# Order edges for the weight decoding of a fused attention and two-layer expert kernel

## The chip, the cores and the metric

The kernel runs on one core of a Trainium2 chip. The metric is the device time of one execution in microseconds. A core has five engines that each work through their own instructions in order: TensorE (PE; its weight loads are shown apart as PEld), VectorE (DVE), ScalarE (ACT), GpSimd (POOL) and SyncE (SP), which issues the DMAs. An engine waits for another through semaphores.

## The reference

Attention over 2 batches, 8 heads, 576 positions and 64 channels, in two parts that are added; a gated layer; a layer of four experts:

```
q_d, k_d, v_d = means of q, k, v over groups of 4 positions
out_up    = repeat(softmax(scale * q_d @ k_d.T) @ v_d, 4)
scores    = where(|i - j| < 4, scale * q @ k.T, -1e9)
x = out_up + softmax(scores) @ v           # 1152 tokens x 512

h = x @ w_in                               # 512 x 2048
x = (h * sigmoid(h)) @ w_out               # 2048 x 512

p = domain_probs / sum(domain_probs)       # 1152 x 4
out = sum over e of p[:, e] * (relu(x @ w1[e]) @ w2[e])    # 512 x 1024, 1024 x 512
```

## The kernel before

**Precision.** Each float32 operand of a large product is kept as two halves, h and l, of TensorE's fast type: h is the rounded value (a copy by ScalarE), l the difference (a subtraction by VectorE or GpSimd). A product is three matmuls, h·h, h·l, l·h (`mm3`).

**Attention** is 16 jobs (2 batches, 2 ranges of 256 and 320 queries, 4 pairs of heads), spread over ticks, three ticks from one job to the next. A job's instructions are: scores L303 and L327 on TensorE; maximum L316, L317, exponent L321, sum L324, downsampled maximum L341 to L343; normalising L348 to L353; transposes L363, L365; values L391, L395; the sum o (L400), and the two halves of x, xh (L407, ScalarE) and xl (L408, VectorE). Four jobs make one chunk of tokens; chunks have 256, 320, 256 and 320 tokens.

**Layer one** has two halves of 1024 hidden channels (`hf`), four chunks each, and in each chunk eight first steps (`g1_step`: 12 matmuls at L468, evacuated by L487 on ScalarE, L488 on VectorE and, one step later, by L493 and L494) and four second steps (`g2_step`: 24 matmuls at L468, evacuated by L520 in the first half, by L523, L525 and a ScalarE copy in the second). The attention of later chunks runs among the steps of earlier ones.

**Weights of layer one** come as eight units (0 to 7) of four pieces. Units 0 and 1 are the first weights of half 0, units 2 and 3 its second weights. A piece is loaded into one of three `stg` buffers and decoded (`split_raw`): two ScalarE steps (L165, L166), two VectorE steps on `dec` (L167, L169; `dec` has two buffers), h by ScalarE (L171), l by GpSimd (L172). When a piece has been taken, the next load is given out. Units 8 and 9, two pieces each, are plain float32, the first half of expert 0's weights: h by L175, l by L176. The text counts units from one where it says "units two to four", which are 1 to 3 in the code; pieces are counted from one, so units 1 to 3 are pieces 5 to 16.

**Layer two** goes through four experts, four chunks and four steps. First products are again L468 (`m1_products`), evacuated by L644; sums `r` (L649), their halves L651 and L652; then seven products at L667 on weights in the form of sums: `ks` (L568) holds sums of the raw weights `kst`, and `split_kk` makes halves of sums and weights (L596, L598).

**What sets the order.** The code is written in program order with a priority for each instruction (`prio`, `at_prio`; ticks and steps are its unit), and a scheduler with a model of the engines' times places instructions on the engines by priority and readiness. A piece is decoded at priority `needed(u, j) - LEAD_SPLIT` and loaded at `needed(u, j) - LEAD_LOAD`; `SPLIT_AT` says at which ticks of the attention the first ten pieces are called. Later pieces are called by `split_ok` after a step, as long as their unit is under `limit`. A manual edge without a semaphore ("NoSync") only says that an instruction stands behind another one.

## Time and profile before

| | |
|---|---|
| Runs | 705.44, 707.71, 708.93 us; median 707.71 |
| Profiled execution | 708.98 us, its span from first to last instruction 707.20 us |
| Granted TensorE clock, mean | 0.984 of full speed |
| PE busy | 668.5 us (95%) |
| PEld busy | 649.8 us (92%) |
| DVE busy | 445.1 us (63%) |
| ACT busy | 332.6 us (47%) |
| POOL busy | 248.9 us (35%) |
| DMA | 48.16 MB |

In the trace the first chunk's steps end near 98.7 us, the third chunk begins near 148, the second half of layer one near 212, layer two near 312, and the last products near 700. A busy time by stretch gives for each engine the busy microseconds and, in brackets, the number of instructions; PEclk is the granted TensorE clock as a share of full speed. In a timeline or a chain the columns are start, length, engine, line, operation, tiles and shapes; neighbouring instructions of one kind are joined (x2), and a bracket says how long the engine had been idle before and which engine, tile and line released it. A mean over a line is over instructions with different neighbours.

### The profile page before, as it was taken

The numbers are of one execution on the slowest core, as the hardware profiler recorded it, in microseconds if no ns is written. First come the engines' busy times: TensorE is split into PE (matmuls) and PEld (weight loads), VectorE is DVE, ScalarE is ACT, GpSimd is POOL, SyncE is SP. The second block draws the span as 40 slices with busy tenths as digits, with TensorE's granted clock in tenths as the row PEclk, the third lists the DMA queues.
The fourth block names the chain that finished last, engine by engine and source line by source line (L and its number), as shares of the span: only waits on it lengthen the run. The fifth ranks groups of instructions, "written<-read, shape, count | busy, mean of one in ns | idle before, by whom it ended". The sixth has DMA issues, their size and how long they took to land.

```text
span 707.2 us, 13791 instructions
## 1 busy us (share of the span) xinstructions
PE 668.5 (95%) x5516; PEld 649.8 (92%) x5516; DVE 445.1 (63%) x882; ACT 332.6 (47%) x753; POOL 248.9 (35%) x346
## 2 busy tenths in 40 slices
PE   5777999999989999998999999999999999999996
PEld 4565899999889999998999999999999999999995
DVE  5988747546864434674555886538866559755444
ACT  4667646457763422543334643335533356433321
POOL 4574442114420000365324482136542244322210
PEclk9978999999999999999999999999999999999999
DMA  9875532005461000032001420003210010000001
GB/s 260 246 220 196 164 94 64 22 12 168 137 201 32 1 1 1 1 123 87 1 1 33 139 69 1 1 1 112 99 31 1 1 53 9 1 32 16 17 31 44
DMA packets 16927, 48.16 MB, mean 68 GB/s; under 512 B 2976, under 2 KB 4256, under 8 KB 16864
## 3 DMA queue, kind: packets, MB, share of 16 engines
q1 hardware_dynamic: 16864, 47.29, 21.4%
q8 instruction: 43, 0.70, 0.4%
q14 instruction: 20, 0.16, 0.1%
HBM read 44.93 MB, written 2.36 MB: 67 GB/s over the span
## 4 chain that ended last, share of the span: by engine, by line
PE 79%; DMA 8%; DVE 6%; ACT 3%; issue 2%; POOL 2%; SPq 0%; DVEq 0%; POOLq 0%; ACTq 0%
PE mm L468 49%; PE p L667 25%; DMA stg<-in_w_dram 5%; DVE dec L169 2%; DMA kst<-in_w2d_dram 2%; DVE dec L167 1%; PE s L303 1%; POOL wbuf L172 1%; DMA vg<-in_va_dram 1%; PE o L395 1%; PE t L363 1%; ACT dec L165 1%; PE o L391 1%; DVE gl L494 1%; ACT stg L166 1%
## 5 line engine op out<-in xcount | busy, mean ns | idle before, releaser
L468 PE MATMUL mm<-xh,wbuf 128*128 128x256 f32 (+2 forms) x1280 | 274.6, 299 | 5.5 <-ACT xh L407 2.8
L468 PEld LDWEIGHTS mm<-xh,wbuf 128*128 128x128 f32 x1280 | 214.2, 192 | 7.2 <-DVE gf L488 3.6
L468 PE MATMUL mm<-xl,wbuf 128*128 128x256 f32 (+2 forms) x640 | 191.0, 299 | 0.0
L649 POOL TENSOR_TENSOR r<-r 128x128 f32<-128x128 f32 x160 | 93.5, 595 | 190.9 <-ACT r L644 150.9
L652 DVE TENSOR_TENSOR h<-r,h 128x384 fp32r<-128x384 f32 (+1 forms) x128 | 89.8, 702 | 72.5 <-ACT h L651 72.2
L468 PEld LDWEIGHTS mm<-xl,wbuf 128*128 128x128 f32 x640 | 122.5, 191 | 0.3
L651 ACT ACTIVATE h<-r 128x384 fp32r<-128x384 f32 (+1 forms) x128 | 73.9, 578 | 87.2 <-POOL r L649 57.2
L468 PE MATMUL mm<-gh,wbuf 128*128 128x256 f32 (+1 forms) x512 | 104.7, 297 | 0.9 <-ACT acc L520 0.9
L667 PE MATMUL p<-wext,h 128*128 128x256 f32 x672 | 96.1, 284 | 2.4 <-ACT h L651 2.4
L667 PEld LDWEIGHTS p<-wext,h 128*128 128x128 f32 x672 | 87.6, 191 | 2.8 <-ACT h L651 2.8
L667 PE MATMUL p<-wbuf,h 128*128 128x256 f32 x672 | 85.4, 280 | 0.0
L468 PEld LDWEIGHTS mm<-gh,wbuf 128*128 128x128 f32 x512 | 82.6, 188 | 1.2 <-ACT acc L520 1.2
L667 PEld LDWEIGHTS p<-wbuf,h 128*128 128x128 f32 x672 | 82.0, 188 | 0.0
L468 PE MATMUL mm<-gl,wbuf 128*128 128x256 f32 (+1 forms) x256 | 74.6, 297 | 0.0
L644 ACT ACTIVATE r<-mm 128x512 f32<-128x512 f32 x48 | 28.6, 597 | 82.4 <-PE mm L468 82.4
L649 DVE TENSOR_TENSOR r<-r 128x128 f32<-128x128 f32 x96 | 33.4, 348 | 40.7 <-ACT r L644 36.3
L494 DVE TENSOR_TENSOR gl<-gf,gh 128x256 fp32r<-128x256 f32 (+1 forms) x64 | 35.9, 562 | 19.6 <-ACT gh L493 19.4
L468 PEld LDWEIGHTS mm<-gl,wbuf 128*128 128x128 f32 x256 | 47.8, 188 | 0.1
L172 POOL TENSOR_TENSOR wbuf<-dec,wbuf 128x512 fp32r<-128x512 f32 x24 | 32.4, 1354 | 33.1 <-ACT wbuf L171 26.0
L598 POOL TENSOR_TENSOR wext<-kst,wext 128x512 fp32r<-128x512 f32 x8 | 10.6, 1325 | 85.0 <-issue 72.9
L695 DVE SCALAR_TENSOR_TENSOR acc<-p,pr,acc 128x256 f32<-128x256 f32 (+1 forms) x63 | 36.3, 604 | 6.5 <-PE p L667 6.5
L493 ACT ACTIVATE gh<-gf 128x256 fp32r<-128x256 f32 (+1 forms) x64 | 28.2, 441 | 19.0 <-DVE gf L488 19.0
(122 smaller groups left out, 989.0 us busy)
## 6 DMA issues: line engine op xcount, KB each, us to landing
stg<-in_w_dram SPq DMA_DIRECT2D x32, 512.0 KB
kst<-in_w2d_dram SPq DMA_DIRECT2D x16, 512.0 KB
kst<-in_w1d_dram SPq DMA_DIRECT2D x12, 512.0 KB
kq<-in_kqa_dram SPq DMA_DIRECT2D x8, 419.0 KB
kq<-in_kqb_dram SPq DMA_DIRECT2D x8, 323.0 KB
vg<-in_va_dram SPq DMA_DIRECT2D x8, 288.0 KB
stg<-in_w1d_dram SPq DMA_DIRECT2D x4, 512.0 KB
vw<-in_vb_dram SPq DMA_DIRECT2D x8, 180.0 KB
```

Of the source, the lines that this page charges most:

```text
L169: DVE.scalar_tensor_tensor(out=ai, in0=v[:, :, 1], scalar=-2 ** 31, in1=ai, op0=ALU.bitwise_and, op1=ALU.bitwise_or)
L172: POOL.tensor_tensor(out=l[:, c], in0=a, in1=h[:, c].bitcast(F32), op=ALU.subtract)
L468: ins = [PE.matmul(out=ps, lhsT=l, rhs=r, start=(first and i == 0), stop=(last and i == n - 1)) for i, (l, r) in enumerate(pairs)]
L493: ACT.activation(out=gh[ft][:, 0:n], in_=gf[:, 0:n], func=ACTF.Copy)
L494: DVE.tensor_tensor(out=gl[ft][:, 0:n], in0=gf[:, 0:n], in1=gh[ft][:, 0:n].bitcast(F32), op=ALU.subtract)
L598: eng.tensor_tensor(out=l[:, r], in0=x, in1=h[:, r].bitcast(F32), op=ALU.subtract)
L644: ACT.activation(out=r[:, 0:4].rearrange("p s t -> p (s t)"), in_=ps[:, 0:512], func=ACTF.Relu)
L649: (DVE if k in FAST_K and o != 7 else POOL).tensor_tensor(out=r[:, o], in0=r[:, a], in1=r[:, b], op=op)
L651: ACT.activation(out=h, in_=r[:, part], func=ACTF.Copy)
L652: DVE.tensor_tensor(out=l, in0=r[:, part], in1=h.bitcast(F32), op=ALU.subtract)
L667: ins = [PE.matmul(out=ps, lhsT=x, rhs=y, start=(opens and k == 0 and i == 0), stop=(k == 3 and i == n - 1), skip_group_check=True) for i, ...
L695: DVE.scalar_tensor_tensor(out=o, in0=ps, scalar=p, in1=o, op0=ALU.mult, op1=ALU.add)
```

## The change

In the first chunk the pieces of units 1 to 3 get other priorities (`needed`), other ticks (`SPLIT_AT`), and an edge: their first VectorE step stands behind the xl subtraction (L408) of an attention job, behind job 2's for unit 1 and behind job 3's for units 2 and 3 (jobs count from 0). In the second half, the pieces of units 8 and 9 are no longer called at the end of the fourth chunk of half 0 but behind odd first steps of the second chunk of half 1, and what counts as background (these pieces, the sums `ks`, the weight halves of expert 0's last two steps) gets an edge behind the running step's last evacuation on its engine (`latest`, `behind`). The sums `ks` are no longer made as soon as a buffer is free in `stage_ahead` but called by name in `sum_ahead`: expert 0's together with the weight halves, a later expert's in the third chunk and behind `split_kk`.

```diff
-SPLIT_AT = (-14, -11, -8, -6, -5, -5, -4, -3, -2, -1)
+SPLIT_AT = (-14, -11, -8, -6, -4, -4, -4, -4, -1, -1)
...
-            return (4, 8, 8, 48, 52, 56, 56)[u - 1]
+            return (-5, -2, 2, 48, 52, 56, 56)[u - 1]
...
+    latest = {}
+    def follow(i, earlier, reason):
+        tc.add_manual_dep(i.ins, earlier.ins.name, mybir.DependencyInfo(mybir.DependencyClass.NoSync, mybir.DependencyReason.DATA),
+                          reason=reason)
+    def behind(eng, i):
+        if eng in latest:
+            follow(i, latest[eng], "background work")
+        return i
...
-            DVE.scalar_tensor_tensor(out=ai, in0=ai, scalar=3, in1=v[:, :, 0],
-                                     op0=ALU.logical_shift_left, op1=ALU.bitwise_or)
+            i = DVE.scalar_tensor_tensor(out=ai, in0=ai, scalar=3, in1=v[:, :, 0],
+                                         op0=ALU.logical_shift_left, op1=ALU.bitwise_or)
+            if u in behind_job:
+                follow(i, behind_job[u], "first weights")
...
-            ACT.activation(out=h[:, c], in_=t, func=ACTF.Copy)
-            DVE.tensor_tensor(out=l[:, c], in0=t, in1=h[:, c].bitcast(F32), op=ALU.subtract)
+            behind(ACT, ACT.activation(out=h[:, c], in_=t, func=ACTF.Copy))
+            behind(DVE, DVE.tensor_tensor(out=l[:, c], in0=t, in1=h[:, c].bitcast(F32), op=ALU.subtract))
...
+        if j.i < 4:
+            behind_job.update({1: i} if j.i < 3 else {2: i, 3: i})
...
-        while sums_todo and sums_todo[0] in staged and ks_p and len(sums) < 2:
+    def sum_ahead(e, k):
+        if (e, k) in ((e, k) for e, x, k in sums_todo):
+            assert sums_todo[0] == (e, "k", k) and len(sums) < 2
...
-                    eng.tensor_tensor(out=o, in0=a, in1=b, op=ALU.subtract)
+                    behind(eng, eng.tensor_tensor(out=o, in0=a, in1=b, op=ALU.subtract))
...
+                if e == 0 and k > 1:
+                    behind(ACT, a)
+                    behind(eng, b)
...
-                split_ok(limit[0])
+                if hf == 1 and ci == 1 and ft % 2:
+                    limit[0] = 10
+                    split_ok(10)
+                elif limit[0] < 10:
+                    split_ok(limit[0])
...
-                for k in range(2):
-                    split_kk(0, k)
+                for k in range(4):
+                    sum_ahead(0, k)
+                    if k < 2:
+                        split_kk(0, k)
...
-                limit[0] = 8 if hf == 0 else 10
+                limit[0] = 8
...
-            if hf == 0 and ci == 3:
-                limit[0] = 10
...
             split_kk(e + 1, k)
+            if k < 2:
+                sum_ahead(e + 1, k + 2)
...
+                if ci == 2 and k % 2 == 0 and e < NE - 1:
+                    sum_ahead(e + 1, k // 2)
```

`latest` is set at L493, L494, L525 and its ScalarE copy, L649 and L652. The order listings below give instructions of one engine in the order in which they stand, with the numbers of the tiles; an instruction's line in after is its line there (L167 and L169 become L180 and L184, L176 becomes L191, L488 and L494 become L504 and L510, L523 and L525 become L539 and L541, L568 becomes L587, L598 becomes L617, L649 becomes L672, L652 becomes L675).

**VectorE, attention of jobs 0 to 2.** `dec` tiles are decoding steps; `o_249` is the sum of job 0, `o_434` of job 2. Before:

```order
L169 SCALAR_TENSOR_TENSOR dec_501<-stg64_403,dec_501 128x512
L167 SCALAR_TENSOR_TENSOR dec_542<-dec_542,stg64_485 128x512
L169 SCALAR_TENSOR_TENSOR dec_542<-stg64_485,dec_542 128x512
L400 TENSOR_TENSOR o_249<-o_249,od_262 128x256
L167 SCALAR_TENSOR_TENSOR dec_590<-dec_590,stg64_499 128x512
L169 SCALAR_TENSOR_TENSOR dec_590<-stg64_499,dec_590 128x512
L341 TENSOR_REDUCE st_280<-s_270 128x1
L408 TENSOR_TENSOR xl_74<-o_249,xh_73 128x256
```

After, on the same engine, from job 0's sum, and from job 2's:

```order
L414 TENSOR_TENSOR o_249<-o_249,od_262 128x256
L422 TENSOR_TENSOR xl_74<-o_249,xh_73 128x256
L355 TENSOR_REDUCE st_280<-s_270 128x1
...
L414 TENSOR_TENSOR o_434<-o_434,od_447 128x256
L355 TENSOR_REDUCE st_467<-s_455 128x1
L330 TENSOR_REDUCE st_593<-s_581 128x5
L356 TENSOR_SCALAR st_467<-st_467 128x1
L422 TENSOR_TENSOR xl_74<-o_434,xh_73 128x256
L180 SCALAR_TENSOR_TENSOR dec_524<-dec_524,stg64_327 128x512
```

The decoding steps that stood around job 0's sum and halves are gone from there; the first of units 1 to 3 (`stg64_327`) now stands behind job 2's xl.

**VectorE, end of half 0's decoding.** `dec_2625` is the last piece of unit 7, `gf_2648` the first evacuation of half 1, the L176 are pieces of units 8 and 9. Before:

```order
L169 SCALAR_TENSOR_TENSOR dec_2625<-stg64_2579,dec_2625 128x512
L176 TENSOR_TENSOR wbuf_76<-stg_2588,wbuf_76 128x1024
L176 TENSOR_TENSOR wbuf_76<-stg_2623,wbuf_76 128x1024
L176 TENSOR_TENSOR wbuf_76<-stg_2632,wbuf_76 128x1024
L488 SCALAR_TENSOR_TENSOR gf_2648<-th_2647,mm_2634 128x256
L176 TENSOR_TENSOR wbuf_76<-stg_2653,wbuf_76 128x1024
L494 TENSOR_TENSOR gl0_85<-gf_2648,gh0_77 128x256
```

After, the same place, and then the first two pieces of units 8 and 9 in the second chunk of half 1:

```order
L184 SCALAR_TENSOR_TENSOR dec_2625<-stg64_2579,dec_2625 128x512
L504 SCALAR_TENSOR_TENSOR gf_2648<-th_2647,mm_2634 128x256
L510 TENSOR_TENSOR gl0_85<-gf_2648,gh0_77 128x256
...
L510 TENSOR_TENSOR gl0_85<-gf_2916,gh0_77 128x320
L191 TENSOR_TENSOR wbuf_76<-stg_2588,wbuf_76 128x1024
L504 SCALAR_TENSOR_TENSOR gf_2933<-th_2932,mm_2919 128x320
L504 SCALAR_TENSOR_TENSOR gf_2956<-th_2955,mm_2942 128x320
L510 TENSOR_TENSOR gl1_86<-gf_2933,gh1_78 128x320
L510 TENSOR_TENSOR gl2_87<-gf_2956,gh2_79 128x320
L191 TENSOR_TENSOR wbuf_76<-stg_2623,wbuf_76 128x1024
```

Four subtractions of 128x1024 have left the place ahead of half 1's first two evacuations and stand one chunk later.

**VectorE and GpSimd, seam of the layers.** L598 are weight halves of expert 0, L523 and L525 the last two evacuations of layer one, L652 the first halves of layer two. VectorE before:

```order
L523 SCALAR_TENSOR_TENSOR gf_3733<-mm_3708,acc_75 128x320
L598 TENSOR_TENSOR wbuf_76<-ks_3630,wbuf_76 128x256
L525 TENSOR_TENSOR xl_74<-gf_3733,xh_73 128x320
L598 TENSOR_TENSOR wbuf_76<-ks_3630,wbuf_76 128x512
L598 TENSOR_TENSOR wbuf_76<-kst_2722,wbuf_76 128x512
L598 TENSOR_TENSOR wbuf_76<-ks_3645,wbuf_76 128x256
L598 TENSOR_TENSOR wbuf_76<-ks_3645,wbuf_76 128x512
L523 SCALAR_TENSOR_TENSOR gf_3762<-mm_3737,acc_75 128x320
L598 TENSOR_TENSOR wbuf_76<-kst_3628,wbuf_76 128x512
L525 TENSOR_TENSOR xl_74<-gf_3762,xh_73 128x320
L652 TENSOR_TENSOR h1_3822<-r_3820,h0_3821 128x384
```

VectorE after:

```order
L539 SCALAR_TENSOR_TENSOR gf_3733<-mm_3708,acc_75 128x320
L541 TENSOR_TENSOR xl_74<-gf_3733,xh_73 128x320
L539 SCALAR_TENSOR_TENSOR gf_3762<-mm_3737,acc_75 128x320
L541 TENSOR_TENSOR xl_74<-gf_3762,xh_73 128x320
L617 TENSOR_TENSOR wbuf_76<-ks_3640,wbuf_76 128x512
L617 TENSOR_TENSOR wbuf_76<-kst_3066,wbuf_76 128x512
L617 TENSOR_TENSOR wbuf_76<-ks_3640,wbuf_76 128x256
L617 TENSOR_TENSOR wbuf_76<-ks_3645,wbuf_76 128x512
L617 TENSOR_TENSOR wbuf_76<-kst_3623,wbuf_76 128x512
L617 TENSOR_TENSOR wbuf_76<-ks_3645,wbuf_76 128x256
L675 TENSOR_TENSOR h1_3812<-r_3810,h0_3811 128x384
```

The six weight halves stood between the evacuations of the last two steps and now stand behind both.

GpSimd before; `ks_3800` and `ks_3815` are sums for expert 1:

```order
L598 TENSOR_TENSOR wbuf_76<-kst_3628,wbuf_76 128x512
L649 TENSOR_TENSOR r_3820<-r_3820 128x128 x4
L649 TENSOR_TENSOR r_3857<-r_3857 128x128 x3
L568 TENSOR_TENSOR ks_3800<-kst_3786 128x256
L568 TENSOR_TENSOR ks_3815<-kst_3798 128x256
L649 TENSOR_TENSOR r_3857<-r_3857 128x128
L568 TENSOR_TENSOR kst_3786<-kst_3786 128x256
```

GpSimd after:

```order
L617 TENSOR_TENSOR wbuf_76<-kst_3623,wbuf_76 128x512
L672 TENSOR_TENSOR r_3810<-r_3810 128x128 x2
L672 TENSOR_TENSOR r_3847<-r_3847 128x128 x2
L672 TENSOR_TENSOR r_3810<-r_3810 128x128
L672 TENSOR_TENSOR r_3847<-r_3847 128x128
L672 TENSOR_TENSOR r_3810<-r_3810 128x128
L672 TENSOR_TENSOR r_3847<-r_3847 128x128
L672 TENSOR_TENSOR r_3909<-r_3909 128x128
```

The sums for expert 1 have left the first steps of expert 0; the first of them comes later in that expert.

## Rows read from the trace of the kernel before

**Rows 1.** Busy time by stretch: stretch, length, engines with instructions, PEclk, DMA share, GB/s.

```profile
20.00:46.00 26.00, 21.38 (x181) 17.03 (x183) 22.77 (x39) 17.14 (x42) 15.54 (x14) 0.87 0.77 232
46.00:66.00 20.00, 12.35 (x119) 9.52 (x113) 17.07 (x38) 14.46 (x37) 12.61 (x17) 0.74 0.62 198
70.00:80.00 10.00, 10.00 (x113) 9.28 (x113) 9.35 (x26) 8.24 (x25) 4.37 (x5) 1.00 0.59 187
99.00:150.00 51.00, 51.00 (x570) 46.15 (x570) 30.73 (x85) 27.35 (x82) 11.15 (x27) 1.00 0.14 38
178.00:220.00 42.00, 37.53 (x269) 36.14 (x268) 30.15 (x50) 28.60 (x60) 12.99 (x9) 1.00 0.48 151
220.00:310.00 90.00, 90.00 (x673) 90.00 (x672) 45.36 (x92) 33.59 (x76) 12.25 (x14) 1.00 0.04 13
310.00:330.00 20.00, 17.65 (x131) 17.16 (x131) 11.87 (x15) 6.92 (x14) 14.03 (x19) 0.91 0.39 132
330.00:700.00 370.00, 370.00 (x2936) 370.00 (x2934) 230.08 (x443) 153.41 (x320) 137.19 (x198) 1.00 0.10 31
```

**Rows 2.** VectorE's timeline, sixteenth piece; and a piece's load in the chain.

```profile
67.85 1.80 DVE L169 SCALAR_TENSOR_TENSOR dec<-stg,dec 128x512 int32<-128x512 int32 x1
27.75 4.08 DMA stg<-in_w_dram
```

**Rows 3.** TensorE's timeline in the first chunk's attention; brackets: idle before, and releaser.

```profile
33.63 0.51 PE L327 MATMUL s<-kd,qbd 128*128 128x144 f32 x2 [0.96 <-ACT s L321]
35.84 1.01 PE L468 MATMUL mm<-xh,wbuf 128*128 128x256 f32 x3 [1.69 <-ACT xh L407]
38.06 0.70 PE L391 MATMUL o<-atd,vd 72*64 72x64 f32 x8 [1.21 <-DVE st L342]
48.99 1.02 PE L363 MATMUL t<-ident,sm 128*70 128x128 f32 x4 [2.74 <-DVE sm L352]
54.85 0.46 PE L391 MATMUL o<-atd,vd 72*64 72x64 f32 x8 [1.87 <-DVE xl L408]
```

**Rows 4.** Groups to 100 us (L172: whole span): busy us, mean ns | idle before.

```profile
L169 DVE SCALAR_TENSOR_TENSOR dec<-stg,dec 128x512 int32<-128x512 int32 x18 | 20.3, 1125 | 0.2
L167 DVE SCALAR_TENSOR_TENSOR dec<-dec,stg 128x512 int32<-128x512 int32 x18 | 17.0, 946 | 4.7 <-ACT dec L165 2.9 <-ACT stg L166 1.8
L494 DVE TENSOR_TENSOR gl<-gf,gh 128x256 fp32r<-128x256 f32 x8 | 3.4, 422 | 0.0
L172 POOL TENSOR_TENSOR wbuf<-dec,wbuf 128x512 fp32r<-128x512 f32 x24 | 32.4, 1354 | 33.1 <-ACT wbuf L171 26.0
```

**Rows 5.** TensorE's timeline: end of chunk one, start of three; scores from 98.7 to 150.

```profile
97.90 0.40 PE L468 MATMUL mm<-gh,wbuf 128*128 128x256 f32 x2
98.27 0.28 PE L468 MATMUL mm<-gh,wbuf 128*128 128x256 f32 x1
...
147.80 0.28 PE L468 MATMUL mm<-xh,wbuf 128*128 128x256 f32 x1
...
L303 PE MATMUL s<-kq 64*64 64x70 f32 x112 | 5.7, 230 | 0.0
```

**Rows 6.** Timelines of ScalarE and TensorE at the seam of the halves.

```profile
209.22 1.06 ACT L175 ACTIVATE wbuf<-stg 128x1024 fp32r<-128x1024 f32 x1 [1.36 <-DMA stg<-in_w1d_dram]
212.26 0.38 PE L468 MATMUL mm<-xh,u 128*128 128x256 f32 x1 [1.52 <-DVE gf L488]
215.72 0.39 PE L468 MATMUL mm<-xh,u 128*128 128x256 f32 x1 [0.36 <-DVE gf L488]
```

**Rows 7.** Timelines of GpSimd and TensorE at the seam of the layers.

```profile
322.83 1.41 POOL L568 TENSOR_TENSOR ks<-kst 128x256 f32<-128x256 f32 x2 [2.31 <-DMA kst<-in_w2d_dram]
325.36 1.55 PE L667 MATMUL p<-wext,h 128*128 128x256 f32 x6 [1.95 <-ACT h L651]
```

**Rows 8.** Timelines of VectorE and GpSimd, a decoding step and a low half.

```profile
13.13 2.23 DVE L169 SCALAR_TENSOR_TENSOR dec<-stg,dec 128x512 int32<-128x512 int32 x1
13.55 1.26 POOL L172 TENSOR_TENSOR wbuf<-dec,wbuf 128x512 fp32r<-128x512 f32 x1
```

More of the change, by code (lines that the diff above doesn't have):

```diff
@@ L291, in after @@
     def after(i, earlier):
-        tc.add_manual_dep(i.ins, earlier.ins.name, mybir.DependencyInfo(mybir.DependencyClass.NoSync, mybir.DependencyReason.DATA),
-                          reason="PSUM bank")
+        follow(i, earlier, "PSUM bank")
     def local_scores(j):
@@ L648, in first_products @@
                     for o, a, b, op in SUMS:
-                        (DVE if k in FAST_K and o != 7 else POOL).tensor_tensor(out=r[:, o], in0=r[:, a], in1=r[:, b], op=op)
+                        eng = DVE if k in FAST_K and o != 7 else POOL
+                        latest[eng] = eng.tensor_tensor(out=r[:, o], in0=r[:, a], in1=r[:, b], op=op)
                 h, l = (x[:, part.start - 1:part.stop - 1] for x in st.h)
                 ACT.activation(out=h, in_=r[:, part], func=ACTF.Copy)
-                DVE.tensor_tensor(out=l, in0=r[:, part], in1=h.bitcast(F32), op=ALU.subtract)
+                latest[DVE] = DVE.tensor_tensor(out=l, in0=r[:, part], in1=h.bitcast(F32), op=ALU.subtract)
     def bank(i):
```

20 lines of the change are left out of this document (11 added, 9 removed).

## The prediction

> **What bounds the kernel now.** I read the busy times by stretch first. From 330 to 700 us TensorE is busy for 370.00 us of 370.00 at a granted clock of 1.00, and from 99 to 150 for 51.00 of 51.00 [rows 1]: there TensorE is the bound, and no reordering on another engine can shorten those stretches, only spoil them. It has room in three places. Up to 66 us it waits for the attention of the first chunk and runs at a lower clock: 0.87 from 20 to 46, 0.74 from 46 to 66. At the seam of the two halves of the first layer it is busy for 37.53 us of 42 (178 to 220). At the seam of the two layers, 310 to 330, for 17.65 of 20 at a clock of 0.91 [rows 1]. The change acts on all three, so I cost three terms.
>
> VectorE is the second engine to watch: 17.07 us busy of 20 from 46 to 66, and 9.35 of 10 from 70 to 80 [rows 1]. In before the sixteenth decoded piece, the last that the first chunk's second products need, leaves VectorE at 69.65 (67.85 plus 1.80) [rows 2], long before TensorE starts the last product of that chunk at 98.27 [rows 5]. So before decodes early, at the price of a late attention. After does the reverse.
>
> **Part A, the first chunk: what is gained.** By the order listing the pieces of units two to four (pieces 5 to 16) leave the places between the attention instructions of jobs 0 to 2; the first of them now comes behind job 2's L408. TensorE in before has its first layer product at 35.84, after 1.69 us of waiting for ScalarE, and reaches job 3's values at 54.85, with waits for VectorE of 1.21, 2.74 and 1.87 us between [rows 3]. VectorE was at decoding in each. That is 19.0 us, of which 5.8 are waits and 13.2 its own work. Without them it comes to the same point at 34.1 (the end of L327 [rows 3]) plus 13.2, that is 47.3 instead of 54.85. Ends: 44.6 if the clock is full in that work (13.2 times 0.80, the middle of 0.87 and 0.74), 53.1 if as much waiting remains. I take 47.3, since the order leaves nothing of decoding ahead of these instructions on VectorE.
>
> **Part A: what is paid.** Twelve pieces are now undecoded when job 3's values start. From there to the sixteenth piece the new order has 90 VectorE instructions: 24 decoding ones, 12 of 1.125 and 12 of 0.946 us, 24.9 in all; 16 of evacuation at 0.42, 6.6; [rows 4]; and 50 of attention, 18.5 at 0.37 (the mean of the 85 instructions from 99 to 150, where nothing is decoded, is 30.73 over 85, 0.36 [rows 1]). The sum is 50.0 us; neighbours overlap by some 0.08 us each (an estimate, from starts against ends in the timeline), so 42.8 us of VectorE time. VectorE is busy for 85% of the time from 46 to 66 and 94% from 70 to 80 [rows 1]; at 90% the 42.8 take 47.6 us. The low half on GpSimd, 1.35 us [rows 4], follows. The sixteenth piece is usable at 47.3 + 47.6 + 1.4 = 96.3; ends 88.8 (44.6, and no gap) and 104.9 (53.1, and 85%).
>
> What is left behind that point? I compare with before at the end of its first chunk, 98.55 (98.27 plus 0.28 [rows 5]). By the order listing, where after needs the whole sixteenth piece it has 27 first-chunk products more to do, at 0.12 us (three starts in 0.37 [rows 5]) 3.2 us, and two sets of scores and two of transposes fewer, at 0.95 a set (5.7 us in six sets [rows 5]; transposes taken like them) 3.8 us. The rest is the same, and TensorE is never idle in it, so the break-even is a sixteenth piece at 98.55 + 3.8 − 3.2 = 99.1. At 96.3 **part A gains 2.8 us**. The lower end is 99.1 − 104.9 = −5.8. The upper end is set by TensorE: at before's pace it takes 98.55 − 54.85 + 0.6 = 44.3 us from job 3's values, so it is there at 91.6 at best, 7.5 gained; until the forecast's 96.3 it waits for decoding.
>
> The loads move too. On SP the load of piece 8 now stands behind the window loads of jobs 4 and 5, and so behind job 3's values. It is issued near 49 and takes 4.1 us [rows 2]; VectorE asks for it 8.5 us of work behind 47.3, so near 56. The cover is 3 us; without it at most 4 us are lost, which lies inside the ends. ScalarE holds one first step of piece 7 ahead of job 2's attention; its load was issued at the same place in before.
>
> **Part B, the seam of the halves.** The four pieces of units 9 and 10 (L175, L176) go from the end of the fourth chunk to the second chunk of the next half, behind the running step. In before ScalarE stood at L175 for a load 1.36 us at 209.22, VectorE behind it, and TensorE waited 1.52 us at 212.26 for an evacuation [rows 6]. I take that wait, a smaller one of 0.4 behind it, and 0.6 of the rest, since attention ends some five steps earlier in TensorE's order and decoding of the second half can begin sooner: **2.5 us**; ends 0 (another wait follows) and the whole idle time, 4.5 [rows 1]. At the new place four copies lie beside TensorE steps that leave VectorE more than half free (45.36 us busy of 90 from 220 to 310 [rows 1]); they cost nothing there, and if that cover were gone about 1 us each.
>
> **Part C, the seam of the layers.** In before GpSimd had sums of the next expert (L568) ahead of the running step's L649; it stood 2.31 us for their load at 322.83, and TensorE waited 1.95 us at 325.36 [rows 7]. The sums leave that place, and on VectorE the last step's L523 and L525 come ahead of the weight halves that stood before them. Idle time (2.35 us) and lost clock (17.65 times 0.09, 1.6 us) make 3.9 us at most [rows 1]. But six weight halves now stand ahead of the first L652 on VectorE, about 4 us, and two on GpSimd ahead of the first sums. I take half, **2.0 us**; ends 0 and 3.9. In the other experts sums move among GpSimd instructions that keep it busy for 137 us of 370 [rows 1]: nothing, as long as TensorE stays full.
>
> The edges add no semaphore, only an order on one engine; what is queued behind a moved piece is the next evacuation.
>
> **Sum.** 2.8 + 2.5 + 2.0 = 7.3 us. The profiled execution took 708.98 (span 707.20 and 1.78 around it): 701.7. The median of the runs is 707.71, 1.3 lower, which gives 700.4. I put 701.0.
>
> **Rivals.** (1) The first chunk trades one wait for another: the sixteenth piece comes between 98 and 101 and only B and C remain, 4.5 us or less, so 703 to 708, about 705. For it: twelve pieces in a row on an engine that is already 85 to 94% busy [rows 1]. Against it: 47.3 plus 42.8 plus 1.4 is 91.5, 7.6 us ahead of the break-even.
> (2) **Slower**: decoding becomes the bound of the first chunk because VectorE and GpSimd block each other. A decode instruction that began at 13.13, and beside which GpSimd did a whole low half (13.55, 1.26), took 2.23 us against a mean of 1.125 [rows 4, 8]. After packs the twelve pieces, their GpSimd halves and the key sums of jobs 5 to 9 into one stretch. If each pair costs 3.1 us instead of 2.07, that is 12.4 more, VectorE has 55.2, at 85% 65 us: the sixteenth piece at 113.7, part A loses 14.6, and even with B and C the total is 10.1 slower, 718. It decides from a sixteenth piece at about 107: 99.1 plus the 4.5 of B and C plus half a per cent. Against it: the mean of rows 4 already holds contention at GpSimd's present share of time.
> The Trainium skill speaks for this rival: "SBUF — State Buffer", section "Who interferes with whom", says that a VectorE instruction with two SBUF inputs contends with a GpSimd one that reads SBUF, and the one that comes second is blocked fully. The trace's row of 2.23 us agrees with that.
> (3) Larger gain: VectorE runs without gaps, the sixteenth piece comes at 91.6 or before, and B and C give nearly all: 7.5 + 4 + 4, about 693. For it: 9.35 of 10 [rows 1].
> That the order is not as stated is ruled out by the listing.
>
> **Chances.** Forecast (698 to 704) 0.45; rival 1 0.28; rival 2 0.15; rival 3 0.12. Half a per cent (3.5 us) is about what a measurement of this kernel can tell from no change. The forecast and rival 3 count as faster; of rival 1 0.10 is faster and 0.18 the same, of rival 2 0.02 the same and 0.13 slower: faster 0.67, same 0.20, slower 0.13. The range runs from 692 to 711: it leaves out most of rival 2 and the far end of rival 3.
>
> **What would show it.** Right: job 3's values on TensorE near 48, the sixteenth L169 (by its new line) near 95, the third chunk's first product, which is at 147.80 in before [rows 5], near 145, no wait near the seam at 210, none for the next expert's load at the seam of the layers. Wrong: VectorE below 85% busy between 47 and 95, decode pairs well over 2.1 us there, a clock under 0.9 there, or idle time on TensorE behind 330.

## The result and the profile after

The changed kernel takes 697.61 us (median of four runs, 695.18 to 700.17), the kernel before 708.11: a ratio of 0.9863, 95% interval 0.9824 to 0.9901. The prediction was 701.0, between 692 and 711, faster. The direction and the range were right. The gain is 9.7 us by the ratio, where 7.3 had been forecast. Of its three terms, measured one by one below, one was too large, one about right and one less than half of what it was.

The profiled execution of after took 700.17, its span 698.2: it is the slowest of its four runs. Against the profile of before (708.98) it is 8.8 us shorter; the medians are 10.5 apart. The experiments come back to that difference. In the lines of after, L484 is the old L468, L503 the old L487, L536 the old L520, L666 the old L644, L184 and L187 the old L169 and L172. Each other kernel has line numbers of its own.

Busy time of after by stretch, columns as in [rows 1]; the last stretch ends at 690:

```profile
20.00:46.00 26.00, 22.03 (x229) 17.98 (x227) 15.80 (x40) 12.39 (x35) 10.48 (x17) 0.74 0.52 155
46.00:66.00 20.00, 15.65 (x157) 14.04 (x156) 18.28 (x41) 16.50 (x43) 10.35 (x14) 0.83 0.62 184
70.00:80.00 10.00, 8.39 (x88) 7.37 (x90) 10.00 (x19) 6.46 (x18) 7.30 (x9) 0.83 0.38 120
99.00:150.00 51.00, 51.00 (x545) 47.43 (x544) 29.12 (x83) 28.43 (x84) 7.75 (x20) 0.97 0.15 45
178.00:220.00 42.00, 41.60 (x309) 40.55 (x308) 25.05 (x44) 24.40 (x54) 11.20 (x8) 1.00 0.25 76
220.00:310.00 90.00, 90.00 (x673) 90.00 (x672) 50.94 (x97) 38.33 (x84) 14.67 (x16) 1.00 0.14 42
310.00:330.00 20.00, 20.00 (x170) 20.00 (x169) 11.71 (x20) 8.25 (x17) 9.37 (x15) 1.00 0.27 105
330.00:690.00 360.00, 360.00 (x2851) 360.00 (x2850) 227.26 (x433) 148.79 (x312) 138.35 (x200) 1.00 0.10 32
```

Both seams are full now: TensorE has 41.60 of 42 us where it had 37.53, and 20.00 of 20 at a clock of 1.00 where it had 17.65 at 0.91 [rows 1]. Behind 330 TensorE is as full as it was, as forecast. The first chunk is another matter. From 70 to 80 VectorE is busy for the whole ten microseconds and TensorE for 8.39, where before it had all ten. The granted clock from 20 to 46 is lower too, 0.74 against 0.87 [rows 1].

How much was won where is read from ScalarE's evacuations, which are the same ones in both kernels. Starts in us, worked out by counting them along ScalarE's timeline:

| | before | after | earlier by |
|---|---|---|---|
| first evacuation of layer one | 65.38 | 54.68 | 10.7 |
| first evacuation of the third chunk | 150.67 | 151.60 | −0.9 |
| last first-step evacuation of the fourth chunk | 192.25 | 191.57 | 0.7 |
| first evacuation of the third chunk, second half | 259.95 | 255.77 | 4.2 |
| ninth evacuation of layer two | 356.91 | 348.21 | 8.7 |

So in this execution the first chunk wins 10.7 us of attention and gives all of it back. The third and fourth chunk give 1.6, the seam of the halves about 3.5, the seam of the layers 4.5, and layer two runs in parallel with before at 8.7 us ahead.

Where the first chunk gives it back is read in four timelines of after (start, length, engine, line; brackets: idle before and releaser). TensorE, job 3's values and the fourth second step:

```profile
44.00 0.46 PE L405 MATMUL o<-atd,vd 72*64 72x64 f32 x8 [0.20 <-DVE xl L422]
98.21 0.40 PE L484 MATMUL mm<-gh,wbuf 128*128 128x256 f32 x1 [2.04 <-ACT acc L536]
```

VectorE's second decoding step of the sixteenth piece:

```profile
89.93 0.68 DVE L184 SCALAR_TENSOR_TENSOR dec<-stg,dec 128x512 int32<-128x512 int32 x1
```

GpSimd's low half of that piece:

```profile
92.73 1.28 POOL L187 TENSOR_TENSOR wbuf<-dec,wbuf 128x512 fp32r<-128x512 f32 x1
```

ScalarE, ahead of the first chunk's second-step evacuations:

```profile
96.67 0.66 ACT L179 ACTIVATE stg<-stg 128x512 int32<-128x512 uint16 x1 [2.36 <-DMA stg<-in_w_dram]
97.24 0.64 ACT L178 ACTIVATE dec<-stg 128x512 f32<-128x512 f32 x1
97.78 0.92 ACT L536 ACTIVATE acc<-mm 128x256 f32<-128x256 f32 x3
```

Job 3's values start at 44.00 (before: 54.85 [rows 3]). The sixteenth L184 starts at 89.93 and its low half ends at 94.01 (92.73 plus 1.28), so the piece is there before the 99.1 that the prediction took as the break-even. But ScalarE stands 2.36 us for the load of a later piece, of unit 5, with the three L536 queued behind it; the fourth second step's products wait for one of these accumulators, 2.04 us. Behind that idle time the granted clock is 0.57 for four microseconds, by the busy times of after in short stretches:

```profile
96.00:98.00 2.00, 0.17 (x6) 0.03 (x2) 0.09 (x1) 1.33 (x3) 1.44 (x4) 1.00 0.69 177
98.00:102.00 4.00, 3.79 (x19) 3.79 (x20) 3.04 (x5) 2.89 (x9) 3.40 (x5) 0.57 0.40 120
```

The clock costs 4 times 0.43, 1.7 us. Wait and clock together are 3.7.

### The profile page after: what moved, and what is told of

It is laid out like the page before. It is cut to its first block, busy times and chain, and to the rows that moved or that the text cites. A ratio compares the mean times of both kernels' runs of the same rounds, so it can differ in the third digit from the quotient of the medians.

```text
span 698.2 us, 13803 instructions
## 1 busy us (share of the span) xinstructions
PE 664.5 (95%) x5516; PEld 648.4 (93%) x5516; DVE 443.2 (63%) x882; ACT 331.7 (48%) x753; POOL 247.0 (35%) x346
## 3 DMA queue, kind: packets, MB, share of 16 engines
HBM read 44.93 MB, written 2.36 MB: 68 GB/s over the span
## 4 chain that ended last, share of the span: by engine, by line
PE 85%; DVE 7%; DMA 3%; ACT 2%; issue 1%; POOL 0%; SPq 0%; ACTq 0%; DVEq 0%
PE mm L484 53%; PE p L690 26%; DMA stg<-in_w_dram 3%; DVE dec L180 2%; PE s L317 1%; DVE dec L184 1%; PE t L377 1%; DVE gl L510 1%; PE o L409 1%; PE o L405 1%; PE s L281 1%; DVE acc L718 1%; ACT stg L179 0%; PE s L341 0%; DVE gf L504 0%
## 5 line engine op out<-in xcount | busy, mean ns | idle before, releaser
L484 PE MATMUL mm<-xh,wbuf 128*128 128x256 f32 (+2 forms) x1280 | 271.5, 298 | 3.6 <-ACT xh L421 2.9
L484 PEld LDWEIGHTS mm<-xh,wbuf 128*128 128x128 f32 x1280 | 212.6, 191 | 4.7 <-ACT xh L421 3.5
L484 PE MATMUL mm<-xl,wbuf 128*128 128x256 f32 (+2 forms) x640 | 190.7, 298 | 0.0
L672 POOL TENSOR_TENSOR r<-r 128x128 f32<-128x128 f32 x160 | 93.0, 594 | 189.6 <-ACT r L666 149.9
L675 DVE TENSOR_TENSOR h<-r,h 128x384 fp32r<-128x384 f32 (+1 forms) x128 | 91.5, 717 | 65.8 <-ACT h L674 65.5
L484 PEld LDWEIGHTS mm<-xl,wbuf 128*128 128x128 f32 x640 | 122.5, 191 | 0.1
L484 PE MATMUL mm<-gh,wbuf 128*128 128x256 f32 (+1 forms) x512 | 108.3, 302 | 5.3 <-DVE gf L504 2.1
L690 PE MATMUL p<-wext,h 128*128 128x256 f32 x672 | 93.3, 282 | 0.0
L484 PEld LDWEIGHTS mm<-gh,wbuf 128*128 128x128 f32 x512 | 84.7, 192 | 6.8 <-DVE gf L504 2.5
L690 PEld LDWEIGHTS p<-wext,h 128*128 128x128 f32 x672 | 86.0, 188 | 0.0
L484 PE MATMUL mm<-gl,wbuf 128*128 128x256 f32 (+1 forms) x256 | 75.7, 300 | 0.2 <-DVE gl L510 0.2
L666 ACT ACTIVATE r<-mm 128x512 f32<-128x512 f32 x48 | 28.7, 598 | 82.3 <-PE mm L484 82.0
L672 DVE TENSOR_TENSOR r<-r 128x128 f32<-128x128 f32 x96 | 33.4, 348 | 41.1 <-ACT r L666 36.6
L484 PEld LDWEIGHTS mm<-gl,wbuf 128*128 128x128 f32 x256 | 49.0, 192 | 0.5 <-DVE gl L510 0.5
L510 DVE TENSOR_TENSOR gl<-gf,gh 128x256 fp32r<-128x256 f32 (+1 forms) x64 | 33.8, 533 | 17.8 <-ACT gh L509 16.6
L187 POOL TENSOR_TENSOR wbuf<-dec,wbuf 128x512 fp32r<-128x512 f32 x24 | 31.9, 1337 | 30.3 <-ACT wbuf L186 19.3
L617 POOL TENSOR_TENSOR wext<-kst,wext 128x512 fp32r<-128x512 f32 x8 | 10.6, 1324 | 82.7 <-ACT wext L615 44.7
L504 DVE SCALAR_TENSOR_TENSOR gf<-th,mm 128x256 f32<-128x256 f32 (+1 forms) x64 | 28.5, 449 | 13.5 <-ACT th L503 12.7
```

The lines of the kernel that those rows point to most:

```text
L187: POOL.tensor_tensor(out=l[:, c], in0=a, in1=h[:, c].bitcast(F32), op=ALU.subtract)
L484: ins = [PE.matmul(out=ps, lhsT=l, rhs=r, start=(first and i == 0), stop=(last and i == n - 1)) for i, (l, r) in enumerate(pairs)]
L504: DVE.scalar_tensor_tensor(out=gf[:, 0:n], in0=th[:, 0:n], scalar=1.0, in1=ps[:, 0:n], op0=ALU.add, op1=ALU.mult)
L510: latest[DVE] = DVE.tensor_tensor(out=gl[ft][:, 0:n], in0=gf[:, 0:n], in1=gh[ft][:, 0:n].bitcast(F32), op=ALU.subtract)
L617: b = eng.tensor_tensor(out=l[:, r], in0=x, in1=h[:, r].bitcast(F32), op=ALU.subtract)
L666: ACT.activation(out=r[:, 0:4].rearrange("p s t -> p (s t)"), in_=ps[:, 0:512], func=ACTF.Relu)
```

## The experiments

The order in which the instructions stand settles one thing without a run. With the edges taken out, the new table and the new due times give the order of before, row for row on all five engines; with the edges kept and the old table and due times put back, the order of after. The edges of units 3 and 4 change nothing either once unit 2's stands behind job 2, since the pieces follow one another through their buffers. The whole first-chunk part is the one edge of unit 2's pieces behind job 2. In the same way the moved calls at the seam of the halves change nothing without their edges. And each of the three parts moves only its own stretch of the program, so they can be run apart.

### The three parts alone

Each is the kernel before with one part of the change. First chunk only: the table, `needed` and this.

```diff
+            if u in behind_job:
+                follow(i, behind_job[u], "first weights")
...
+        if j.i < 4:
+            behind_job.update({1: i} if j.i < 3 else {2: i, 3: i})
```

> The first-chunk part alone: the kernel before with the new table, the new due times and the edges behind jobs 2 and 3. Theory 1 (the three terms add): by the evacuations of the two traces the fourth chunk's first steps, which still lie ahead of the moved pieces of units 9 and 10, end 0.7 to 1.0 us earlier in after, so this kernel gains about 0.9 us, ratio 0.9987, the same within the noise. Theory 2 (the term of the prediction): 2.8 us, ratio 0.996. Theory 3 (the seam of the halves takes it back, because VectorE and ScalarE stand there for loads that come no earlier): 0 us at the end, with the first chunk's early steps 10 us earlier all the same.

Measured: 706.01 against 709.15, ratio 0.997 (0.9945 to 0.9995). The twelve runs fall into two heaps: seven from 703.6 to 706.4, five from 709.5 to 711.2. The profiled one is the fastest; its order of instructions up to the seam is that of after, and yet its third chunk's first evacuation starts at 145.90, not at 151.60. No wait for an L536 is in it. So the same order gains 4.8 us in one execution and loses 0.9 in another, and the mean, 2.1 us by the ratio (0.4 to 3.9), lies between theories 1 and 2 and does not decide between them. Theory 3 falls: in this profile the last first-step evacuation of the fourth chunk is 6.9 us earlier than in before (185.38) and the first of the second half's third chunk 7.0 (252.97), so the seam of the halves takes nothing back.

Seam of the halves only:

```diff
+            behind(ACT, ACT.activation(out=h[:, c], in_=t, func=ACTF.Copy))
+            behind(DVE, DVE.tensor_tensor(out=l[:, c], in0=t, in1=h[:, c].bitcast(F32), op=ALU.subtract))
...
+                if hf == 1 and ci == 1 and ft % 2:
+                    limit[0] = 10
+                    split_ok(10)
```

> The seam of the halves alone: units 9 and 10 behind the running step of the second half's second chunk. Theory 1: 3.3 us (evacuations go from 0.8 to 4.2 us earlier there between the two traces), ratio 0.995. Theory 3 (this part only pays because the first chunk's change lets decoding of the second half begin earlier): 1.9 us, the two waits of 1.52 and 0.36 us, and no more. Prediction: 2.5 us.

Measured: 706.64, ratio 0.9957 (0.9937 to 0.9978), that is 3.0 us. What TensorE still waits for from 178 to 220 in this kernel (columns: engine, line, releaser: us in total, times, longest):

```profile
PE mm L482 <- DVE gf L502: 1.2, 2, 1.0
PE mm L482 <- ACT acc L534: 0.9, 1, 0.9
```

Of the 4.5 us of idle time there [rows 1], 2.1 are left. The last first-step evacuation of the fourth chunk is 0.7 us later than in before (192.96), the first of the second half's third chunk 2.2 earlier (257.75), which makes 2.9. So theory 1 fits best, though theory 3's 1.9 us lies inside the interval (1.6 to 4.5 us); the first chunk's change is not needed for most of this gain.

Seam of the layers only:

```diff
+    def sum_ahead(e, k):
...
+                    behind(eng, eng.tensor_tensor(out=o, in0=a, in1=b, op=ALU.subtract))
...
+                if e == 0 and k > 1:
+                    behind(ACT, a)
+                    behind(eng, b)
```

> The seam of the layers alone: sums and weight halves behind the running step. Theory 1: 4.5 us (evacuations go from 4.2 to 8.7 us earlier between the two traces), ratio 0.9936: 2.4 us of waits in products of L667, 1.7 of lower clock behind the longer one, and 0.4 ahead of it. Rival: the half of it that the prediction took, 2.0 us, and the rest of the 4.5 belongs to the other parts, because TensorE reaches the seam earlier with them.

Measured: 704.38, ratio 0.9933 (0.9917 to 0.995), 4.8 us. Its seam, same columns as [rows 1]:

```profile
310.00:330.00 20.00, 20.00 (x169) 20.00 (x168) 13.25 (x23) 10.55 (x21) 8.71 (x12) 1.00 0.36 132
```

Theory 1 holds (the interval is 3.5 to 5.9 us); the rival's 2.0 lies outside it. The product of the three ratios is 0.986, the ratio of the whole: the parts add.

### After once more, and without the first-chunk part

> The changed kernel once more, unchanged, as the measure for the next three. The three parts alone gave 0.997, 0.9957 and 0.9933; if they add, their product 0.986 comes again. Theory 1 (the first chunk's gain depends on how VectorE's decoding steps fall among GpSimd's instructions, which differs from run to run): the runs spread over 5 us or more, as those of the first-chunk part alone did (703.6 to 711.2), and the first chunk of this profile ends by some us earlier or later than in the profile after, with the same order of instructions. Rival (the profile after is typical): spread under 3 us, the third chunk's first steps again near 152.

Measured: 700.25 (695.82 to 702.17, six runs), ratio 0.986 (0.9835 to 0.9886). The spread is 6.4 us, and the profiled execution, 695.82, has its third chunk at 147.74, 3.9 us earlier than the other profile of the same kernel. The spread that theory 1 expected is there, and so is the difference between two executions of one order. The two profiles differ in two places. The first is a decoding step, that of the twelfth piece. VectorE in the timeline of the first profile of after:

```profile
71.36 2.54 DVE L184 SCALAR_TENSOR_TENSOR dec<-stg,dec 128x512 int32<-128x512 int32 x1
```

GpSimd there:

```profile
71.08 1.04 POOL L254 TENSOR_TENSOR vg<-vg 72x512 f32<-72x512 f32 x1 [4.07 <-DMA vg<-in_va_dram]
72.08 1.26 POOL L187 TENSOR_TENSOR wbuf<-dec,wbuf 128x512 fp32r<-128x512 f32 x1
```

The same step on VectorE in this execution:

```profile
71.13 0.67 DVE L184 SCALAR_TENSOR_TENSOR dec<-stg,dec 128x512 int32<-128x512 int32 x1
```

And GpSimd's sum:

```profile
71.14 1.56 POOL L254 TENSOR_TENSOR vg<-vg 72x512 f32<-72x512 f32 x1 [3.33 <-DMA vg<-in_va_dram]
```

In the first, GpSimd begins 0.28 us ahead, and VectorE's step ends at 73.90, behind GpSimd's second instruction (73.34). In the second, VectorE begins first, takes 0.67, and GpSimd's sum takes 1.56 instead of 1.04. GpSimd was released by the landing of a load in both. Which of two instructions begins first decides here over 1.9 us of VectorE. The Trainium skill, "SBUF — State Buffer", section "Who interferes with whom", states the rule: issue order decides who blocks. These rows agree. They are no exception: in the first 130 us of the profiles of before, after and this run, 59 decoding steps began while GpSimd did nothing or was within 0.06 us of its end, and each took 0.64 to 0.69 us, also where a GpSimd instruction began beside it. The other 49 began inside a GpSimd instruction and took 0.67 to 2.53, 1.19 in the mean.

The second place is a load. The 2.1 us by which VectorE is behind at 73.81 in the first profile have shrunk to 0.7 at 77.03, and at ScalarE's L421 of 93.89 (here 93.39) only 0.5 are left. Then ScalarE comes to the piece of unit 5 whose wait is shown above, until 96.67. Its load was given out there, and here, at

```profile
90.68 0.33 SPq L153 DMA_DIRECT2D stg<-in_w_dram  x1
90.17 0.33 SPq L153 DMA_DIRECT2D stg<-in_w_dram  x1
```

and here ScalarE takes the piece up at

```profile
94.26 0.71 ACT L179 ACTIVATE stg<-stg 128x512 int32<-128x512 uint16 x1 [0.45 <-DMA stg<-in_w_dram]
```

From the issue to this step it is 6.0 us in the first profile and 4.1 here, and with it the 0.5 us become 2.4. Behind TensorE's wait and its lower clock they are 3.7 (the fourth L536 starts at 103.13 and at 99.40), nearly all of the 3.9. So the two executions part mainly by a load that landed later, and not by the decoding step; why that load took longer is not shown. Nor is it the clock at the start: from 20 to 46 it is 0.74 in the first profile and 1.00 here, but 0.76 in that of only_a, which is the fastest of its runs and has its third chunk at 145.90. The spread is also not after's alone: the 23 runs of before beside the three parts go from 706.57 to 713.54, 7.0 us.

The mean lengths of the two decoding steps between 30 and 100 us (xcount | busy us, mean ns | idle before), the first profile:

```profile
L184 DVE SCALAR_TENSOR_TENSOR dec<-stg,dec 128x512 int32<-128x512 int32 x14 | 12.3, 885 | 0.0
L180 DVE SCALAR_TENSOR_TENSOR dec<-dec,stg 128x512 int32<-128x512 int32 x14 | 12.2, 870 | 2.6 <-ACT dec L178 2.6
```

and this one:

```profile
L184 DVE SCALAR_TENSOR_TENSOR dec<-stg,dec 128x512 int32<-128x512 int32 x14 | 11.2, 805 | 0.0
L180 DVE SCALAR_TENSOR_TENSOR dec<-dec,stg 128x512 int32<-128x512 int32 x14 | 10.8, 770 | 0.8 <-ACT dec L178 0.8
```

A pair takes 1.76 us in the one and 1.58 in the other.

After without the first-chunk part:

```diff
-SPLIT_AT = (-14, -11, -8, -6, -4, -4, -4, -4, -1, -1)
+SPLIT_AT = (-14, -11, -8, -6, -5, -5, -4, -3, -2, -1)
...
-            return (-5, -2, 2, 48, 52, 56, 56)[u - 1]
+            return (4, 8, 8, 48, 52, 56, 56)[u - 1]
...
-        if j.i < 4:
-            behind_job.update({1: i} if j.i < 3 else {2: i, 3: i})
```

> After without the first-chunk part (old table and due times, no edges behind jobs): the two seams alone. If the parts add: 0.9957 times 0.9933, 0.989, so 2 us slower than after, with a smaller spread. Theory that the first chunk's part is worth what the prediction said: 2.8 us slower than after. Theory that it is worth nothing at the end because the seam of the halves takes it back: the same as after within 0.7 us.

Measured: 701.71 (699.93 to 702.82, five runs), ratio 0.9887 (0.9868 to 0.9906): 1.9 us slower than after_again by the ratios, as the sum of the parts says, though the two intervals overlap.

### Is it the wait for unit 5's load?

In after, the products waited for L536 behind a decoding step of unit 5. One more edge keeps that unit back:

```diff
+            if u == 4:
+                for a_i in first:
+                    follow(a_i, last_y[0], "first chunk")
```

(`first` are the two first ScalarE steps, `last_y` the latest L536 of the first chunk.)

> After with one more edge: the first two ScalarE decoding steps of unit 5 (the seventeenth to twentieth piece) stand behind the evacuation of the first chunk's last second step. In after a decoding step of that unit stood on ScalarE for a load until 96.67 us, three evacuations behind it, and TensorE waited 2.04 us at 98.21 for a free accumulator, and then had a granted clock of 0.57 from 98 to 102. Theory 1 (this wait is where the first chunk's gain is lost): 2.0 us of wait and 1.7 us of clock come back, 3.7 us against after, about 694. Rival (the wait is hidden: the time comes back as a later wait for decoding, since the same pieces must be decoded later): within 1 us of after.

Measured: 701.29, ratio 0.9894 (0.9875 to 0.9914), so not faster than after. Theory 1 falls. By the ratios the kernel is 2.4 us slower than after_again, with intervals that overlap, so the rival's "within 1 us" is not decided. The wait of 2.04 us for an accumulator is down to 0.65 in the profile (at 99.53), and another stands in its place. VectorE's timeline of this kernel:

```profile
87.40 3.98 DVE L181 SCALAR_TENSOR_TENSOR dec<-dec,stg 128x512 int32<-128x512 int32 x1
```

GpSimd's, of the same stretch:

```profile
87.35 1.04 POOL L258 TENSOR_TENSOR vg<-vg 72x512 f32<-72x512 f32 x1 [1.15 <-DMA vg<-in_va_dram]
88.34 1.28 POOL L191 TENSOR_TENSOR wbuf<-dec,wbuf 128x512 fp32r<-128x512 f32 x1
89.58 0.63 POOL L258 TENSOR_TENSOR vd<-vg 72x256 f32<-72x256 f32 x1
90.17 1.49 POOL L258 TENSOR_TENSOR kq<-kq 128x288 f32<-128x288 f32 x2
```

A step of 0.68 us began 0.05 us behind GpSimd and took 3.98, nearly as long as GpSimd went on without a gap. TensorE then waited 2.19 us for a later VectorE instruction. So keeping that step back did not bring the time back: the load's wait is one place of several where the first chunk can lose.

### Does GpSimd's work set the length of the decoding steps?

Low halves of units 2 to 4 on VectorE:

```diff
-            POOL.tensor_tensor(out=l[:, c], in0=a, in1=h[:, c].bitcast(F32), op=ALU.subtract)
+            (DVE if 0 < u < 4 else POOL).tensor_tensor(out=l[:, c], in0=a, in1=h[:, c].bitcast(F32), op=ALU.subtract)
```

> After with the low halves of units 2 to 4 subtracted on VectorE instead of GpSimd. VectorE gets twelve instructions of about 0.7 us more (8.2 us), GpSimd twelve of 1.3 less. Theory 1 (the decoding steps are held up by GpSimd): the decoding pairs, 0.88 and 0.91 us in the mean in after, fall to about 0.70 each, 4 to 6 us come back on VectorE, the total lies within 3 us of after and the spread is smaller. Rival (their length is their own, and VectorE's amount of work is what counts): pairs as long as in after, the first chunk 6 to 8 us later, the total about 5 us slower than after.

Measured: 701.96, ratio 0.9892 (0.9873 to 0.9911), the four runs within 1.4 us. The decoding steps and the low halves of this kernel, groups on VectorE from 30 to 100 us:

```profile
L184 DVE SCALAR_TENSOR_TENSOR dec<-stg,dec 128x512 int32<-128x512 int32 x14 | 10.9, 787 | 0.0
L180 DVE SCALAR_TENSOR_TENSOR dec<-dec,stg 128x512 int32<-128x512 int32 x14 | 10.4, 750 | 6.2 <-ACT dec L178 4.0 <-ACT stg L179 2.2
L187 DVE TENSOR_TENSOR wbuf<-dec,wbuf 128x512 fp32r<-128x512 f32 x12 | 8.2, 694 | 0.0
```

The pair is 1.54 us, hardly below after_again's 1.58 and far above the 1.40 expected. Total and spread came out as theory 1 says, the pair did not. What is left to hold VectorE up would be the rest of GpSimd's work, the sums of keys and values; no run here takes those away.

Each of these low halves computed twice on GpSimd:

```diff
+            for _ in range(2 if 0 < u < 4 else 1):
+                POOL.tensor_tensor(out=l[:, c], in0=a, in1=h[:, c].bitcast(F32), op=ALU.subtract)
```

> After with each GpSimd low half of units 2 to 4 computed twice: twelve more GpSimd instructions of about 1.3 us in the first chunk, VectorE's work unchanged. If GpSimd's instructions hold up VectorE's: the decoding pair on VectorE (1.58 us with no low halves on GpSimd, 1.58 to 1.76 in the two profiles of after) rises to 2.0 us or more, VectorE is held up for 4 us or more in the first chunk, and the total is 3 us or more longer than after. If they do not: the pair stays near 1.7, and the total is longer by what the last low half itself comes later, 1.3 us, and no more.

Measured: 735.44, ratio 1.0416 (1.0328 to 1.0504), some 39 us longer than after by the ratios. The decoding steps, same view:

```profile
L180 DVE SCALAR_TENSOR_TENSOR dec<-dec,stg 128x512 int32<-128x512 int32 x10 | 10.9, 1087 | 1.9 <-ACT dec L178 1.9
L184 DVE SCALAR_TENSOR_TENSOR dec<-stg,dec 128x512 int32<-128x512 int32 x10 | 9.0, 910 | 0.0
```

The pair rose to 2.00, as the contention theory says. (Without low halves on GpSimd it was 1.54; the 1.58 that the expectation gives for that is after_again's.) But the mean of a pair does not follow GpSimd's work alone: with the work of after it is 1.58 and 1.76, but 1.99 in unit4_late (1091 and 898 ns) and 1.81 in the next kernel, edge_job1 (894 and 917 ns), which is faster than after. What shows the contention is the single steps above. And twelve pairs at 0.3 more are 4 us, not 39. In this kernel the second chunk begins some 30 us later than in before; the doubled instructions also changed the order on every engine, and GpSimd's queue holds the sums that attention needs. The run does not separate these, and this size is left open. It says that GpSimd has little room in the first chunk: 15.6 us more of its work (twelve times 1.3) cost more than twice that.

### Where the edge stands

Behind job 1's halves, for all three units:

```diff
-        if j.i < 4:
-            behind_job.update({1: i} if j.i < 3 else {2: i, 3: i})
+        if j.i < 2:
+            behind_job.update({1: i, 2: i, 3: i})
```

> After with the edges behind job 1's halves instead of job 2's and 3's, so that decoding of units 2 to 4 begins one job earlier. If the sixteenth piece is what the first chunk waits for: it is decoded about 5 us earlier than in after, TensorE's accumulators come free earlier, and the total is 2 to 4 us shorter than after. If the attention of jobs 2 and 3 is what counts (the gain of the edges): the first tanh comes 3 to 6 us later than in after, and the total is the same or up to 3 us longer.

Measured: 696.47 (696.23 to 696.86, four runs), ratio 0.9816 (0.9794 to 0.9837), against 0.986 (0.9835 to 0.9886) for after_again on the same chip: about 3 us faster, the intervals just touching, and a spread of 0.6 us. The sixteenth piece on VectorE:

```profile
83.13 0.69 DVE L184 SCALAR_TENSOR_TENSOR dec<-stg,dec 128x512 int32<-128x512 int32 x1
```

It is 6.8 us earlier than in after, the first evacuation is at 53.92, no later than in after (54.68), and the third chunk's at 145.98. The accumulators come free earlier too: the first L536 starts at 88.64, in after at 97.78. The first theory holds. Attention loses nothing by it; VectorE had room, 15.80 us busy of 26 from 20 to 46 in after. But the third chunk's start is that of only_a's profile (145.90), which has the edges of after, so a part of the 3 us may be that the slow executions did not come up in four runs. The runs do not separate this.

Behind job 0's halves (the same diff with `j.i < 1`):

> After with the edge behind job 0's halves, one job earlier than in the run edge_job1 (0.9816, 696.5 us). If the sixteenth piece is all that counts, it is decoded earlier still and the total falls by 1 to 3 us more. If job 1's point is a balance between attention and decoding: the first tanh comes 3 to 5 us later than with job 1, and the total is 1 to 4 us longer than there.

Measured: 696.88, ratio 0.9837 (0.9809 to 0.9865), not to be told from job 1. The first evacuation starts some 5.6 us later than with job 1 (59.6), the third chunk's at 145.86, the same: a balance, and a flat one.

Job 1's edge together with the edge that keeps unit 5 back:

> The edge behind job 1 (0.9816, 696.5 us) together with the edge of the run unit4_late (unit 5's first ScalarE steps behind the first chunk's last evacuation). If a decoding step that waits on ScalarE for a load ahead of an evacuation still costs there: 1 to 3 us shorter. If, as with the edges of after, keeping unit 5 back only moves the wait: the same or up to 3 us longer.

Measured: 694.94 (693.42 to 696.93), ratio 0.9805 (0.9773 to 0.9837): the fastest of all kernels here, though not told from job 1's edge alone by the intervals. Which of the two theories holds stays open.

### Which edge mattered at the seam of the layers

After, with the edges of the weight halves taken out and those of the sums kept:

```diff
-                if e == 0 and k > 1:
-                    behind(ACT, a)
-                    behind(eng, b)
```

> After without the edges of expert 0's last weight halves (the sums keep theirs): on VectorE the six weight halves stand again between the evacuations of layer one's last two steps, on GpSimd the sums for expert 1 stay where after has them. If the wait of GpSimd for a load (2.31 us in before) is the whole of the seam of the layers: the same as after, 0.986, with no wait of TensorE on L674 and the seam's clock at 1.00. If the weight halves ahead of the evacuation matter: about 2 to 4 us slower than after, with TensorE waiting at the seam for ScalarE or VectorE.

Measured: 699.7, ratio 0.9865 (0.9839 to 0.9891), the same as after. TensorE's waits from 290 to 340 in it:

```profile
PE p L687 <- ACT h L671: 0.4, 1, 0.4
```

So the sums were the seam. By this profile the place of the six weight halves is worth at most the 0.4 us of this wait; the interval alone leaves room for about 2 us.

## Why the prediction was right, and where its steps were not

**Part A, 2.8 us: the gain came, its sum was right by luck.** It measured 2.1 us alone (1.9 as the difference of after_again and no_a), with executions from −0.9 to 4.8. VectorE's work held: from job 3's values to the usable sixteenth piece it took 50.0 us (49.0 forecast), with VectorE 91% busy (90%). Three other steps did not.

The start was 44.00, just before the forecast's early end of 44.6, which stood for a full clock: from 34 to 44 us the granted clock is 1.00 in after, and from 36 to 55 in before it is 0.75. So the sixteenth piece came at 94.0, 93.5 and 91.9 in the profiles of after, after_again and only_a, not at 96.3. (Of the three waits that were to go, the one of 2.74 us in before was not spent at decoding: VectorE's L169 ended at 46.09, and until 48.84 it did the attention's own L316 to L352.)

The step that failed most is the break-even, in "The rest is the same". Between the point where the sixteenth piece is needed and the third chunk's first product, after also does two sets of values more than before does behind its 98.55. The groups of values, in before from 98.55 to 147.80 and in after from 94.70 to 149.93 (busy us, mean ns | idle before):

```profile
L395 PE MATMUL o<-at,vw 70*64 70x64 f32 x104 | 4.1, 223 | 0.0
L391 PE MATMUL o<-atd,vd 72*64 72x80 f32 x16 | 1.0, 245 | 0.0
```

```profile
L409 PE MATMUL o<-at,vw 70*64 70x64 f32 x144 | 5.6, 222 | 0.0
L405 PE MATMUL o<-atd,vd 72*64 72x80 f32 x32 | 2.0, 245 | 0.0
```

These are 2.5 us, so the break-even was near 96.6 and not 99.1. With it the forecast's 96.3 would have gained 0.3 us. That the piece came earlier and that the break-even lay earlier nearly cancelled.

Then "TensorE is never idle in it": in the profile of after TensorE waited 2.04 us for an accumulator behind the sixteenth piece and lost 1.7 to the clock. From 96.6 the sums come out: 96.6 − 94.0 − 3.7 is −1.1 (measured −0.9); for after_again 96.6 − 93.5, less a wait of 0.2, is 2.9 (2.9); for only_a 96.6 − 91.9 is 4.7 (4.8). Also missed was that a mean instruction length from one execution stood for something that varies: a decoding step's length depends on who begins first, VectorE or GpSimd.

**Rival 2's mechanism is real, its verdict was not.** VectorE and GpSimd do hold each other up, by 1.9 and 3.3 us at single steps. But the prediction feared that the pairs would rise from 2.07 to 3.1; they fell to 1.58 and 1.76, where the decoding steps stand at other places in GpSimd's stream. The mean of [rows 4] already held the contention of before, which was the larger one. The row of 2.23 us in [rows 8] is read with the GpSimd instruction before the low half, since the low half began behind the step:

```profile
12.63 0.96 POOL L239 TENSOR_TENSOR vd<-vg 72x256 f32<-72x256 f32 x1
```

This one was under way at 13.13, and the low half followed it without a gap.

**Part B, 2.5 us: right.** It measured 3.0 (1.6 to 4.5) alone. In after the waits named [rows 6] are gone and 0.4 us of idle time is left at the seam; four copies in the second chunk cost nothing, and TensorE has all of 220 to 310.

**Part C, 2.0 us: the wrong half.** It measured 4.8 (3.5 to 5.9) alone, above the upper end of 3.9, though the interval reaches below it. The step that failed is "I take half", for the six weight halves that now stand ahead of the first halves of layer two. c_no_split_edge, where they stand ahead of the evacuation again, takes the same time as after: their place is not a cost. The sum should have been the whole of the idle time and the lost clock, 3.9; the 0.9 above it is within the interval and was not found in a row. The clock of before had been read right, as a mean of 0.91 over 310 to 330; in a finer stretch of before it is a clock of 0.66 for five microseconds, right behind the wait of 1.95 us [rows 7], which is 1.7 us:

```profile
325.00:330.00 5.00, 4.64 (x26) 4.64 (x27) 4.14 (x5) 1.71 (x4) 5.00 (x7) 0.66 0.00 0
```

**The rest.** Nothing was lost in layer two, as forecast: the ninth evacuation is 8.7 us earlier, and an evacuation near the end, at 648.86 instead of 657.56, still 8.7. Of the signs that the prediction named, two came out against it in the first profile of after: the clock from 47 to 95 is 0.89, and the third chunk's first product, forecast near 145, starts later than in before (146.08 in after_again):

```profile
149.94 0.28 PE L484 MATMUL mm<-xh,wbuf 128*128 128x256 f32 x1
```

## What to carry to other kernels

Where a scheduler places instructions by priority and readiness, due times and the place of a call may change nothing at all: compare the orders first, and look for the one edge that does. Work that an engine does for later belongs behind what it does for the running step, and a wait of 2 us for such work can be paid twice, once as idle time and once as a lower clock behind it. That was so for the waits of 1.95 us in before and 2.04 in after (1.7 us of clock each); behind 1.91 us at 70.15 in after_again and 2.19 at 91.93 in unit4_late the clock stayed at 1.00. Of work that has to be done in a crowded stretch, postpone only as much as the waiting engine gains from: here an edge one job earlier kept the gain at the start and gave back less of it.
